# Scores of tiles 3 to 5: two heads on two groups of 64 rows, 128 columns a product, instead of 128 rows with zero halves and 256 columns

## The chip, the cores and the metric

The kernel runs on one core of one Trainium2 chip. The metric is the device time of one execution in microseconds (us), the median of three runs.

## What is computed

A chunked linear attention over 4 batches, 8 heads, 768 positions (head size 32, state size 16), then a gated feed-forward layer (256 to 1536 to 256, with an RMS norm ahead) and a second feed-forward layer (256 to 1024 to 256) that mixes each position with the one before it. Cut to what matters here:

```python
CB = np.einsum('bhin,bhjn->bhij', Cc, Bc)      # the scores
L = np.exp(cum[:, :, :, None] - cum[:, :, None, :]) * causal
M = CB * L
y = np.einsum('bhij,bhjd->bhid', M, xc) + np.einsum('bhin,bhnd->bhid', Cc, state) * decay_to_i
...
x = moe(y, w_gate, w_val, w_out, rms_g)        # silu(x w_gate) * (x w_val) w_out
out = moe2(x, mu_k, mu_r, w_k, w_v, w_r)       # sigmoid(xr w_r) * (relu(xk w_k)^2 w_v)
```

A score sums over only 16 states; it has to be as good as float32.

## The kernel before

The 768 positions are cut into six tiles, 0 to 5, of 128 positions by 4 batches (512 columns). Stage t runs the first feed-forward layer of tile t (12 units of gate, value and output products, names g, v and x) and then the second layer of tile t - 1 (names kp, v, rps). The attention of tile t + 1 is worked in between the units of the first layer, through `attend`. A big product is made of three rounded products (L748, L749, L750: high by high, low by high, high by low), each 128 rows by 128 columns of weights against 512 columns in the rounded float32 type (F32R, the trace writes both float32 types as f32 for TensorE).

Scores come from two functions. `scores` (L468; tiles 0 to 2) uses plain float32, on four groups of 32 rows; a plain float32 product stands in the trace as two records. `scores_r` (tiles 3 to 5) uses F32R, one record a product. For it `terms` splits B and C into a rounded part and a rest, so that a score is the sum of four terms over 16 states, 64 rows for one head. Tile `Br` holds, for a pair of heads, 4 terms x 2 heads x 16 states on 128 rows; ScalarE (L425) and VectorE (L428) turn it into `Bs`. `Cr` becomes `Cs`, which has for each pair two blocks of 128 columns, one for each head, with zeros on the rows of the other head: two ScalarE instructions (L427) and two VectorE ones (L430) with column masks from `shape_constants`. One product of `scores_r` (L442) then takes the 128 rows of a pair and gives 256 columns, the scores of both heads. Four products make one batch, a set; there are 3 tiles x 4 batches = 12 sets. A set fills two PSUM banks of the pool `patt`, heads 0 to 3 in the first and 4 to 7 in the second. `mask` (L514) multiplies each bank with the decays E.

`load_terms` (L418) fetches Br and Cr ahead, one DMA of 128 rows each, on SP's queue; both have two buffers, and `Bs` and `Cs` one. `Cs` takes its place from the tag "Cs", which `mix` (p1, L823) uses too. The tag "rs", of half its size, holds the spread norm of a tile (`rms_mm` to `xn_f`, L730).

Other products on groups of rows or columns: `y_two` (L569) and `y_four` (L594), plain float32 on two groups of 64 rows, 128 columns each; `y_x` (L527) and `y_st` (L533), on groups of 32 output rows; `spread_e` (L393), F32R on groups of 32 rows with 512 columns. `rms_mm` (L685) makes plain float32 products of 128 rows with one column.

The order on each engine is not written by hand: `arrange` at the end plays the program through with a table of prices (`price`) and fixes the order that comes out. An instruction starts there when its inputs, its place and its engine are free, the earliest in the program first.

Of the kernel before, what the change touches and what calls it, by code (L numbers as in the profile page):

```python
# [9 lines left out]
F32 = mybir.dt.float32  # L10
F32R = mybir.dt.float32r
BF16 = mybir.dt.bfloat16
I32, U32 = mybir.dt.int32, mybir.dt.uint32
AF = mybir.ActivationFunctionType
ALU = mybir.AluOpType

P = 128
NB, NH, S, D, N = 4, 8, 768, 32, 16
# [3 lines left out]
T = NB * P  # L22

SB, SC0, SC1, MC0, MC1, EPS = range(6)
# [30 lines left out]
def shape_constants():  # L55
    p = np.arange(P)
    k = np.zeros((P, KW), np.float32)
    k[:, EPS] = 1e-6
    term, h2 = p // 32, (p // 16) % 2
    k[:, SB] = np.where(term >= 2, -1.0, 0.0)  # L60
    for j in range(2):
        k[:, MC0 + j] = h2 == j
        k[:, SC0 + j] = np.where((term % 2 == 1) & (h2 == j), -1.0, 0.0)
    for h in range(NH):
        k[:, M8 + h] = (p // N) % 4 == h
    rest, last, head = p % 4 % 2, p % 4 // 2, p // 4 % NH
    k[:, GL] = np.where(rest == 1, -1.0, 0.0)
    k[:, SL], k[:, CL] = np.where(last == 1, -1.0, 0.0), last == 0
    k[:, SR], k[:, CR] = last == 0, last == 1
    for j in range(2):  # L70
        k[:, ML + j] = head // 4 == j
    for h in range(4):
        k[:, MR + h] = head % 4 == h
    return k
# [3 lines left out]
def tile_kernel(ctx: ExitStack, tc, a_c, x_t, B_t, B_s, C_s, B_p, C_p, C_h, kc,  # L78
                w_gate, w_val, w_out, w_k, w_v, w_r, out):
    nc = tc.nc  # L80
    slots, chains, groups, gates, urgent, ranks, costs = {}, [], [], [], [], {}, {}
# [13 lines left out]
    rp = Pool("rp", 1)  # L95
# [3 lines left out]
    patt = Pool("patt", 2, bass.MemoryType.PSUM)  # L99
# [16 lines left out]
    def f32(ap):  # L116
        return ap.bitcast(F32)
# [39 lines left out]
    def kcol(j):  # L157
        return k_sb[:, j:j + 1]
# [63 lines left out]
    for q in range(NU // 2):  # L222
        s = slice(2 * P * q, 2 * P * (q + 1))
# [81 lines left out]
    A = {c: {} for c in range(NC + 2)}  # L305
# [70 lines left out]
    def spread_eye(c, b):  # L376
        for half in range(2):
            pool, tag = (pacc, "acc") if c and b in LATE_E else (pmm, "mm")
            ps = A[c]["Eb", b, half] = pool.tile([P, T], F32, tag=tag, name="Eb")
            mm = nc.tensor.matmul(ps, eye, before.unsqueeze(1).broadcast_to([P, 4, P]), start=True, stop=False)  # L380
            if len(costs) < COLD:
                costs[mm.ins.name] = 427.0
            A[c]["eye", b, half] = mm.ins.name
# [24 lines left out]
    def parity(c):  # L408
        return c == 2

    def load_terms(c, b):
        if b >= NB:
            c, b = c + 1, b - NB
        if c >= NC:
            return
        for nm, src in (("Br", B_s), ("Cr", C_s)):
            r = A[c][nm, b] = rp.tile([P, T], F32, tag=nm, bufs=2, name=nm)
            nc.sync.dma_start(out=r, in_=src[c, b].unsqueeze(0).broadcast_to([4, 32, T]))  # L418

    def terms(c, b):  # L420
        d = A[c]
        bs = d["Bs", b] = rp.tile([P, 4, P], F32R, tag="Bs", bufs=1, name="Bs")
        cs = d["Cs", b] = rp.tile([P, 4, 2, P], F32R, tag="Cs", bufs=1, name="Cs")
        br, cr = (d.pop((nm, b)).rearrange("p (k i) -> p k i", k=4) for nm in ("Br", "Cr"))
        nc.scalar.activation(out=bs, in_=br, func=AF.Copy, scale=kcol(SB))  # L425
        for j in range(2):
            nc.scalar.activation(out=cs[:, :, j, :], in_=cr, func=AF.Copy, scale=kcol(SC0 + j))  # L427
        nc.vector.tensor_add(bs, br, f32(bs))  # L428
        for j in range(2):
            nc.vector.scalar_tensor_tensor(  # L430
                out=cs[:, :, j, :], in0=cr, scalar=kcol(MC0 + j), in1=f32(cs[:, :, j, :]),
                op0=ALU.mult, op1=ALU.add)
        load_terms(c, b + 2)

    def scores_r(c, b):
        d = A[c]
        bs, cs = d.pop(("Bs", b)), d.pop(("Cs", b))
        for half in range(2):
            bank = d["sc", b, half] = patt.tile([P, T], F32, tag="at", name="sc")
            for q in range(2):  # L440
                p = 2 * half + q
                nc.tensor.matmul(bank[:, q * 256:(q + 1) * 256], bs[:, p, :],  # L442
                                 cs[:, p, :, :].rearrange("p a i -> p (a i)"), start=True, stop=True)

    def load16(r, src):
        for g in range(4):
# [21 lines left out]
    def scores(c, two):  # L468
        br, cr = A[c].pop(("B16", two)) if parity(c) else A[c]["B4"][:, two], A[c].pop(("C4", two))
        pools = ((patt, "at"), (pacc, "acc") if (c, two) in SPARE else (pmm, "mm"))  # L470
        banks = [[pool.tile([P, T], F32, tag=tag, name="sc") for _ in range(2)] for pool, tag in pools]
        rows, w, n = (N, P, 4) if parity(c) else (2 * N, 2 * P, 2)
        for k in range(n):
            for j in range(4):
                g = slice(32 * j, 32 * j + rows)
                mm = nc.tensor.matmul(banks[j // 2][j % 2][:, k * w:(k + 1) * w], br[g, k * P:(k + 1) * P], cr[g, k * w:(k + 1) * w],
                                      start=True, stop=True)
                costs[mm.ins.name] = w / 2.0
                if j + k == 0:
                    groups.append((mm.ins.name, [t.name for bank in banks for t in bank]))  # L480
                A[c]["sc", 2 * two + j // 2, j % 2] = banks[j // 2][j % 2]
        if c and two:
            for two in range(2):
                if c == 1:
                    load_bs(c + 1, two)
                    load_c(c + 1, two, nc.sync)
                else:
                    load_terms(c + 1, two)
# [20 lines left out]
    def mask(c, b, half):  # L509
        d = A[c]  # L510
        if c == 0 and ("M", b) not in d:
            d["M", b] = rp.tile([P, NH, P], F32, tag="hl", bufs=pair_bufs["hl"], name="M")
        s = slice(half, NH, 2) if parity(c) else slice(4 * half, 4 * half + 4)
        nc.vector.tensor_mul(d["E" if c else "M", b][:, s, :], d.pop(("sc", b, half)).rearrange("p (h i) -> p h i", h=4), d["E", b][:, s, :])  # L514

    def masked(c, b):
        decayed_b(c, b)
        for half in range(2):
            mask(c, b, half)
# [373 lines left out]
    def warm_up(n, pool, tag):  # L893
        w = pool.tile([P, T], F32, tag=tag, name="warm")
        for k in range(n):
            mm = nc.tensor.matmul(w, ones, ones.unsqueeze(1).broadcast_to([P, 4, P]), start=True, stop=True)
            if len(costs) < COLD:
                costs[mm.ins.name] = 427.0 if costs else 900.0
# [32 lines left out]
    def masks(b):  # L931
        for half in range(2):
            mask(0, b, half)
# [25 lines left out]
    def late_decayed(_):  # L959
        for b in range(NB):  # L960
# [4 lines left out]
                 k=lambda n: (norm_eye, scan_masks)[n](), w=lambda n: warm_up(n, patt, "at"), q=lambda b: spread_eye(0, b))  # L965
    for step in START.split():
        at = len(list(nc.cur_bb.bb.instructions))
# [27 lines left out]
    for t in range(NC):  # L995
        c, e = t + 1, t + 2
# [25 lines left out]
        def attend(u):  # L1022
# [6 lines left out]
            if c > 2 and u in (1, 3, 6, 8):  # L1029
                terms(c, (u + 1) // 3)  # L1030
            if c > 2 and u in at_sc:
                scores_r(c, at_sc.index(u))
                masked(c, at_sc.index(u))
            elif u in at_sc and (c, at_sc.index(u)) not in SPARE:
                two = at_sc.index(u)
                scores(c, two)
                for b in range(2 * two, 2 * two + 2):
                    masked(c, b)
# [373 lines left out]
```

## Time and profile before

| | us |
|---|---|
| median of 3 runs (lowest, highest) | 508.61 (508.54, 508.73) |
| the profiled execution, its own time | 508.6 |
| its span on the engines | 506.6 |
| TensorE (PE) busy | 500.2 |
| VectorE (DVE) busy | 375.7 |
| ScalarE (ACT) busy | 307.9 |

The 2.0 us between the span and the execution's time lie around the program. Busy time of TensorE counts a product from its start to its modelled end, and products follow each other sooner than that: a product of 512 columns is shown with 389 ns, and the next starts 227 ns later. So the cost of a product is read from the distance of starts or from the chain of waits, not from its own length. The granted clock of TensorE was full (1.00 in every stretch).

### The profile page before, as it was taken

The page shows a single profiled execution, that of the slowest core. Times are in us where ns is not written, and L with a number is a line of the kernel's source. Part 1 is how long each engine was busy: PE and PEld are TensorE (multiplying, and loading weights), DVE is VectorE, ACT ScalarE, POOL GpSimd, SP SyncE. Part 2 cuts the span into 40 slices and gives each one's busy share as a digit, 9 for nine tenths or more (in the row PEclk, how much of TensorE's full clock was granted, in tenths as well). Part 3 has the DMA queues.
Part 4 walks back from the last instruction along what each step waited for, and adds up shares of the span by engine and source line. Part 5 has one row for each costly group of instructions (what it writes and reads, how often), then busy time and mean ns, then how long its engine had stood idle before and what let it go on. Part 6 is the DMA issues. An engine that isn't in the chain of part 4 may idle for free.

```text
span 506.6 us, 7497 instructions
## 1 busy us (share of the span) xinstructions
PE 500.2 (99%) x2869; PEld 406.8 (80%) x2869; DVE 375.7 (74%) x610; ACT 307.9 (61%) x509; POOL 10.4 (2%) x26
## 2 busy tenths in 40 slices
PE   8999999999999999999999999999999999999997
PEld 4687887788888888888888888888888888888885
DVE  6899998988698965479995659996628763335672
ACT  5999798566589744457763456764358643345552
POOL 1100000000010000010000010000000000000000
PEclk9999999999999999999999999999999999999999
DMA  8868755342321220152111141110000000000101
GB/s 257 230 204 276 261 175 193 105 137 93 123 85 43 78 82 13 57 174 77 42 58 68 46 162 44 65 48 36 0 1 1 18 25 1 1 1 0 42 0 42
DMA packets 23283, 42.60 MB, mean 84 GB/s; under 512 B 3136, under 2 KB 6720, under 8 KB 23248
## 3 DMA queue, kind: packets, MB, share of 16 engines
q1 hardware_dynamic: 20496, 33.41, 20.0%
q10 hardware_dynamic: 2752, 8.72, 5.1%
q8 instruction: 22, 0.36, 0.3%
q14 instruction: 13, 0.11, 0.1%
HBM read 38.52 MB, written 3.34 MB: 83 GB/s over the span
## 4 chain that ended last, share of the span: by engine, by line
PE 91%; DVE 5%; ACT 2%; issue 1%; DMA 1%; DVEq 0%; ACTq 0%
PE v L748 10%; PE v L750 10%; PE v L749 10%; PE g L748 6%; PE x L748 6%; PE x L749 6%; PE x L750 6%; PE g L749 6%; PE g L750 6%; PE kp L748 4%; PE kp L750 4%; PE kp L749 4%; PE y L527 2%; PE sc L442 1%; PE rps L750 1%; PE rps L749 1%
## 5 line engine op out<-in xcount | busy, mean ns | idle before, releaser
L792 DVE TENSOR_TENSOR hf<-sl,v 128x512 f32<-128x512 f32 x72 | 49.0, 683 | 50.0 <-PE v L750 49.5
L140 ACT CAST h<-hf 128x512 fp32r<-128x512 f32 x72 | 44.4, 617 | 60.8 <-DVE hf L792 60.7
L133 ACT ACTIVATE sl<-g 128x512 f32<-128x512 f32 x72 | 42.8, 595 | 44.9 <-PE g L750 44.6
L143 DVE TENSOR_TENSOR h<-hf,h 128x512 fp32r<-128x512 f32 x72 | 50.5, 701 | 24.1 <-ACT h L140 24.1
L748 PE MATMUL g<-xn,wgh 128*128 128x512 f32 (+1 forms) x148 | 58.0, 392 | 0.4 <-DVE E L514 0.4
L749 PE MATMUL g<-xn,wgl 128*128 128x512 f32 (+1 forms) x148 | 57.0, 385 | 0.4 <-DVE wgl L289 0.4
L748 PE MATMUL v<-xn,wvh 128*128 128x512 f32 (+1 forms) x148 | 57.0, 385 | 0.0
L750 PE MATMUL g<-xn,wgh 128*128 128x512 f32 (+1 forms) x148 | 56.8, 384 | 0.0
L749 PE MATMUL v<-xn,wvl 128*128 128x512 f32 (+1 forms) x148 | 56.8, 384 | 0.0
L750 PE MATMUL v<-xn,wvh 128*128 128x512 f32 (+1 forms) x148 | 56.8, 383 | 0.0
L749 PE MATMUL x<-h,wol 128*128 128x512 f32 x144 | 56.3, 391 | 0.0
L748 PE MATMUL x<-h,woh 128*128 128x512 f32 x144 | 55.8, 391 | 0.1
L750 PE MATMUL x<-h,woh 128*128 128x512 f32 x144 | 55.2, 389 | 0.0
L867 DVE TENSOR_TENSOR k<-rl 128x512 f32<-128x512 f32 x40 | 30.0, 749 | 15.0 <-ACT rl L863 15.0
L143 DVE TENSOR_TENSOR h<-k,h 128x512 fp32r<-128x512 f32 x48 | 32.8, 686 | 10.3 <-ACT h L140 9.9
L140 ACT CAST h<-k 128x512 fp32r<-128x512 f32 x48 | 29.7, 619 | 16.5 <-DVE k L867 16.3
L748 PE MATMUL kp<-xm,wkh 128*128 128x512 f32 x96 | 37.7, 393 | 0.0
L750 PE MATMUL kp<-xm,wkh 128*128 128x512 f32 x96 | 37.4, 390 | 0.0
L749 PE MATMUL kp<-xm,wkl 128*128 128x512 f32 x96 | 37.4, 389 | 0.0
L748 PE MATMUL v<-h,wvvh 128*128 128x512 f32 x96 | 37.3, 389 | 0.0
L749 PE MATMUL v<-h,wvvl 128*128 128x512 f32 x96 | 37.3, 389 | 0.0
L863 ACT ACTIVATE rl<-kp 128x512 f32<-128x512 f32 x48 | 28.5, 594 | 14.1 <-PE kp L750 13.4
(157 smaller groups left out, 983.0 us busy)
## 6 DMA issues: line engine op xcount, KB each, us to landing
E<-la_r ACTq DMA_DIRECT2D x16, 512.0 KB
x<-in_x_t SPq DMA_DIRECT2D x6, 512.0 KB
wst<-in_w_gate SPq DMA_DIRECT2D x6, 512.0 KB
wst<-in_w_val SPq DMA_DIRECT2D x6, 512.0 KB
wst<-in_w_out SPq DMA_DIRECT2D x6, 512.0 KB
Br<-in_B_s SPq DMA_DIRECT2D x12, 256.0 KB
Cr<-in_C_s SPq DMA_DIRECT2D x12, 256.0 KB
out<-r SPq DMA_DIRECT2D x11, 256.0 KB
```

The lines of the kernel that those rows point to most:

```text
L133: one = nc.scalar.activation(out=out, in_=in_, func=func, **kw).ins.name
L140: last[1] = nc.scalar.copy(x[:, 0, :], src).ins
L143: last[0] = le.tensor_tensor(out=x[:, 1, :], in0=src, in1=f32(x[:, 0, :]), op=ALU.subtract).ins
L442: nc.tensor.matmul(bank[:, q * 256:(q + 1) * 256], bs[:, p, :], cs[:, p, :, :].rearrange("p a i -> p (a i)"), start=True, stop=True)
L527: nc.tensor.matmul(y[half][32 * j:32 * j + 32, at[half]:at[half] + P], x[:, b, h * D:(h + 1) * D], m[:, h, :], start=start and at[half] == ...
L748: nc.tensor.matmul(ps[:, s], w[0][:, k, ws], x[:, 0, s], start=first, stop=False, skip_group_check=s.stop - s.start < T)
L749: nc.tensor.matmul(ps[:, s], w[1][:, k, ws], x[:, 0, s], start=False, stop=False, skip_group_check=s.stop - s.start < T)
L750: nc.tensor.matmul(ps[:, s], w[0][:, k, ws], x[:, 1, s], start=False, stop=last, skip_group_check=s.stop - s.start < T)
L792: nc.vector.tensor_mul(hf, sl, v)
L863: marks.append(nc.scalar.activation(out=rl, in_=kp, func=AF.Relu).ins.name)
L867: nc.vector.tensor_mul(k2, rl, rl)
```

## The change

A head gets its own 64 rows. `load_terms` places 4 terms x 16 states of the pair's first head on rows 0 to 63 and those of the second head on rows 64 to 127, with two DMAs of 64 rows for each of Br and Cr. `terms` treats C as it treats B: one ScalarE and one VectorE instruction each; `Cs` has no zero halves, 512 columns instead of 1024, and lies in the place of tag "rs". `scores_r` makes eight products a set (now L434 of the changed file, where lines are shifted by up to 8): for each pair one on rows 0 to 63 and one on rows 64 to 127, each with 128 columns, into two banks, which are now taken together: the first has the even heads, the second the odd ones. `mask` reads the decays with that step for tiles 3 to 5 as it did for tile 2.

```diff
--- before.py
+++ after.py
@@ -56,11 +56,8 @@
     p = np.arange(P)
     k = np.zeros((P, KW), np.float32)
     k[:, EPS] = 1e-6
-    term, h2 = p // 32, (p // 16) % 2
-    k[:, SB] = np.where(term >= 2, -1.0, 0.0)
-    for j in range(2):
-        k[:, MC0 + j] = h2 == j
-        k[:, SC0 + j] = np.where((term % 2 == 1) & (h2 == j), -1.0, 0.0)
+    term = p // N % 4
+    k[:, SB], k[:, SC0] = np.where(term >= 2, -1.0, 0.0), np.where(term % 2 == 1, -1.0, 0.0)
     for h in range(NH):
         k[:, M8 + h] = (p // N) % 4 == h
     rest, last, head = p % 4 % 2, p % 4 // 2, p // 4 % NH
@@ -415,32 +412,29 @@
             return
         for nm, src in (("Br", B_s), ("Cr", C_s)):
             r = A[c][nm, b] = rp.tile([P, T], F32, tag=nm, bufs=2, name=nm)
-            nc.sync.dma_start(out=r, in_=src[c, b].unsqueeze(0).broadcast_to([4, 32, T]))
+            for h in range(2):
+                nc.sync.dma_start(out=r[64 * h:64 * h + 64], in_=src[c, b, N * h:N * h + N].unsqueeze(0).broadcast_to([4, N, T]))
 
     def terms(c, b):
-        d = A[c]
-        bs = d["Bs", b] = rp.tile([P, 4, P], F32R, tag="Bs", bufs=1, name="Bs")
-        cs = d["Cs", b] = rp.tile([P, 4, 2, P], F32R, tag="Cs", bufs=1, name="Cs")
-        br, cr = (d.pop((nm, b)).rearrange("p (k i) -> p k i", k=4) for nm in ("Br", "Cr"))
-        nc.scalar.activation(out=bs, in_=br, func=AF.Copy, scale=kcol(SB))
-        for j in range(2):
-            nc.scalar.activation(out=cs[:, :, j, :], in_=cr, func=AF.Copy, scale=kcol(SC0 + j))
-        nc.vector.tensor_add(bs, br, f32(bs))
-        for j in range(2):
-            nc.vector.scalar_tensor_tensor(
-                out=cs[:, :, j, :], in0=cr, scalar=kcol(MC0 + j), in1=f32(cs[:, :, j, :]),
-                op0=ALU.mult, op1=ALU.add)
+        for nm, tag, k in (("B", "Bs", SB), ("C", "rs", SC0)):
+            r = A[c].pop((nm + "r", b))
+            s = A[c][nm + "s", b] = rp.tile([P, T], F32R, tag=tag, bufs=1, name=nm + "s")
+            nc.scalar.activation(out=s, in_=r, func=AF.Copy, scale=kcol(k))
+            nc.vector.tensor_add(s, r, f32(s))
         load_terms(c, b + 2)
 
     def scores_r(c, b):
         d = A[c]
         bs, cs = d.pop(("Bs", b)), d.pop(("Cs", b))
-        for half in range(2):
-            bank = d["sc", b, half] = patt.tile([P, T], F32, tag="at", name="sc")
-            for q in range(2):
-                p = 2 * half + q
-                nc.tensor.matmul(bank[:, q * 256:(q + 1) * 256], bs[:, p, :],
-                                 cs[:, p, :, :].rearrange("p a i -> p (a i)"), start=True, stop=True)
+        banks = [patt.tile([P, T], F32, tag="at", name="sc") for _ in range(2)]
+        for p in range(4):
+            i = slice(p * P, p * P + P)
+            for j in range(2):
+                g = slice(64 * j, 64 * j + 64)
+                mm = nc.tensor.matmul(banks[j][:, i], bs[g, i], cs[g, i], start=True, stop=True)
+                if j + p == 0:
+                    groups.append((mm.ins.name, [t.name for t in banks]))
+                d["sc", b, j] = banks[j]
 
     def load16(r, src):
         for g in range(4):
@@ -510,7 +504,7 @@
         d = A[c]
         if c == 0 and ("M", b) not in d:
             d["M", b] = rp.tile([P, NH, P], F32, tag="hl", bufs=pair_bufs["hl"], name="M")
-        s = slice(half, NH, 2) if parity(c) else slice(4 * half, 4 * half + 4)
+        s = slice(half, NH, 2) if c > 1 else slice(4 * half, 4 * half + 4)
         nc.vector.tensor_mul(d["E" if c else "M", b][:, s, :], d.pop(("sc", b, half)).rearrange("p (h i) -> p h i", h=4), d["E", b][:, s, :])
 
     def masked(c, b):
```

On TensorE, at the first set (tile 3, batch 0; sc are scores, g and v the first layer's products of stage 2). Before:

```order
L750 MATMUL v<-xn,wvh 128x512
L748 MATMUL g<-xn,wgh 128x512
L749 MATMUL g<-xn,wgl 128x512
L750 MATMUL g<-xn,wgh 128x512
L748 MATMUL g<-xn,wgh 128x512
L749 MATMUL g<-xn,wgl 128x512
L750 MATMUL g<-xn,wgh 128x512
L442 MATMUL sc<-Cs,Bs 128x256 x4
L748 MATMUL v<-xn,wvh 128x512
```

The same place after:

```order
L744 MATMUL v<-xn,wvh 128x512
L434 MATMUL sc<-Cs,Bs 128x128 x8
L742 MATMUL g<-xn,wgh 128x512
L743 MATMUL g<-xn,wgl 128x512
L744 MATMUL g<-xn,wgh 128x512
L742 MATMUL g<-xn,wgh 128x512
L743 MATMUL g<-xn,wgl 128x512
L744 MATMUL g<-xn,wgh 128x512
L742 MATMUL v<-xn,wvh 128x512
```

The set stands six products of 512 columns earlier, and has eight products for four; on both sides of it stand products of 128 rows, as before. The other eleven sets also stand alone between such products.

On VectorE, the same stretch and the next set (hf, h and xm belong to the feed-forward layers, E<-sc is `mask`, Bs and Cs are `terms`). Before:

```order
L143 TENSOR_TENSOR h<-hf,h 128x512
L430 SCALAR_TENSOR_TENSOR Cs<-Cr,k_sb,Cs 128x4x128 x2
L792 TENSOR_TENSOR hf<-sl,v 128x512
L514 TENSOR_TENSOR E<-sc,E 128x512 x2
L143 TENSOR_TENSOR h<-hf,h 128x512
L792 TENSOR_TENSOR hf<-sl,v 128x512
L428 TENSOR_TENSOR Bs<-Br,Bs 128x512
L430 SCALAR_TENSOR_TENSOR Cs<-Cr,k_sb,Cs 128x4x128
```

The same place after:

```order
L140 TENSOR_TENSOR h<-hf,h 128x512
L786 TENSOR_TENSOR hf<-sl,v 128x512
L508 TENSOR_TENSOR E<-sc,E 128x4x128 x2
L140 TENSOR_TENSOR h<-hf,h 128x512
L423 TENSOR_TENSOR Bs<-Br,Bs 128x512
L423 TENSOR_TENSOR Cs<-Cr,Cs 128x512
```

The first set's Cs is no longer here: it stands in the stage before, ahead of `mix`, since its place is no longer that of p1. From the second set on, one Cs instruction follows Bs instead of two.

## Rows read from the trace of the kernel before

**Rows 1.** The page's first part: busy us, share of the span, instructions.

```profile
PE 500.2 (99%) x2869; PEld 406.8 (80%) x2869; DVE 375.7 (74%) x610; ACT 307.9 (61%) x509; POOL 10.4 (2%) x26
```

**Rows 2.** Who waited for whom from 125 us on: total us, times, longest.

```profile
PEld y L594 <- issue: 1.4, 4, 0.4
PEld sc L442 <- issue: 0.4, 2, 0.2
PEld sc L442 <- DVE Cs L430: 0.3, 1, 0.3
```

**Rows 3.** The chain that ended last, 125 to 506 us: start, us, what.

```profile
131.16 1.09 PE y L594 x16
...
173.37 0.63 PE sc L442 x4
...
256.51 0.47 PE sc L442 x4
...
261.54 0.50 PE sc L442 x4
...
341.12 0.51 PE sc L442 x4
```

**Rows 4.** The same chain around the second set, and at the last.

```profile
180.61 0.23 PE x L750
180.84 0.47 PE sc L442 x4
181.31 0.23 PE g L748
...
365.50 0.47 PE sc L442 x4
```

**Rows 5.** The chain around two products on two groups of 64 rows.

```profile
38.11 0.42 PE y L569 x4
38.53 0.43 PE x L749
```

**Rows 6.** The chain around sixteen products on four groups of rows.

```profile
117.59 1.10 PE sc L476 x32
118.70 0.43 PE g L748
```

**Rows 7.** The chain over eight records of one column with 128 rows.

```profile
75.17 0.45 PE x L748 x2
75.62 0.80 PE ss L685 x8
```

**Rows 8.** TensorE's groups by shape: weights, moving data, count, busy us, mean ns, idle.

```profile
L442 PE MATMUL sc<-Cs,Bs 128*128 128x256 f32 x48 | 7.8, 285 | 0.0
L476 PE MATMUL sc<-Cr,Br 16*128 16x128 f32 x64 | 2.3, 283 | 0.0
L569 PE MATMUL y<-Ch,Sf 64*128 64x128 f32 x16 | 1.7, 310 | 0.0
```

**Rows 9.** Timeline of TensorE's weight loads and products: start, us, shape, [idle before].

```profile
38.04 0.30 PEld L569 LDWEIGHTS y<-Ch,Sf 64*128 64x128 f32 x4 [0.36 <-issue]
...
7.70 0.30 PEld L393 LDWEIGHTS Eb<-wvvh,wkh 32*128 32x128 f32 x4 [0.42 <-issue]
...
7.71 0.73 PE L393 MATMUL Eb<-wvvh,wkh 32*128 32x512 f32 x4
```

**Rows 10.** Instructions of `terms`, `mask` and `load_terms`: ns min/median/max, first and last start.

```profile
L427 ACT ACTIVATE Cs<-Cr,k_sb x24: 707/712/722, 169.8 to 358.6; 128x512 fp32r<-128x512 f32 x24
L430 DVE SCALAR_TENSOR_TENSOR Cs<-Cr,k_sb,Cs x24: 742/745/749, 171.8 to 359.4; 128x512 fp32r<-128x512 f32 x24
L428 DVE TENSOR_TENSOR Bs<-Br,Bs x12: 681/683/686, 109.9 to 358.2; 128x512 fp32r<-128x512 f32 x12
L514 DVE TENSOR_TENSOR E<-sc,E x40: 679/683/692, 25.5 to 366.8; 128x512 f32<-128x512 f32 x40
L418 SPq DMA_DIRECT2D Br<-in_B_s x12: 536/545/580, 96.4 to 338.9; - x12
```

## The prediction

> **What bounds the kernel now.** I read the page's busy times first: TensorE is busy for 500.2 of 506.6 us, VectorE for 375.7, ScalarE for 307.9 [rows 1]. So the question is what TensorE has to do, and whether it ever waits. The first instruction that stands elsewhere on TensorE is the first set of scores of tile 3, at 173 us; of the waits from 125 us on, the products have none, and the weight loads wait for another engine once, 0.3 us: the first set, for VectorE's Cs. The rest is "issue", time in which nothing is waited for, mostly ahead of L594 [rows 2]. So in the stretch that the change touches, the kernel is as long as its queue of products, and a microsecond more or less on TensorE is a microsecond of the result. Work that VectorE, ScalarE or a DMA saves there has nothing to give.
>
> Next I read the chain of waits, which says what each set costs on that path. A usual set of four products of 256 columns takes 0.47 us [rows 4], 0.118 us a product. Three sets took longer, 0.63, 0.50 and 0.51 us [rows 3]; the other nine are at 0.47, from 180.84 to 365.50 us [rows 4]. Twelve sets: 1.64 + 9 x 0.47 = 5.87 us. That is all there is to win on the path.
>
> **The change part by part.**
>
> *The products.* A set becomes four steps of two products, one on each group of 64 rows. Two questions decide: what a step costs, and what going to groups of rows and back costs. Both are in the trace for other products.
>
> L569 is two products on two groups of 64 rows with 128 columns [rows 8], the new shape but in plain float32, two records each: two steps of two. It is alone between products of 128 rows, as the new sets are. The chain gives it 0.42 us, and the product behind it 0.43 instead of 0.23 us [rows 5, 4]: 0.62 us in all. L476 for tile 2 is sixteen products of 128 columns on four groups, 32 records, eight steps of four: 1.10 us, and again 0.43 for the product behind, so 1.30 us [rows 6]. Between them lie six steps: (1.30 - 0.62) / 6 = 0.113 us a step, whether two or four products stand side by side. What is left with no step at all is 0.62 - 2 x 0.113 = 0.39 us: the two changes of the array between 128 rows and groups of rows. The 0.20 us behind are half of it. The other half is ahead: the weight loads of L569 begin 0.36 us after the last load ended, put down to "issue" [rows 9], where they otherwise run during the product before. L594, eight steps of two groups of 64 rows, takes 1.09 us on the chain [rows 3], as L476 does, so the number of groups does not matter.
>
> A new set is then 0.39 + 4 x 0.113 = 0.84, with rounding 0.85 us, against 0.47. Twelve: 10.2 us.
>
> Why does a step not get shorter with fewer columns? L685 has records of 128 rows with one column only, and eight of them take 0.80 us on the chain [rows 7], 0.10 a step. So the step is that of the weight load, and 256 columns at 0.118 us were already near it. A set has eight loads instead of four, two of them at a time. From these rows a step is between 0.10 and 0.113 us; I take 0.113, since it comes from steps with groups and 128 columns. The lower end would take 12 x 4 x 0.013 = 0.6 us off.
>
> The Trainium skill states a lower price: TensorE: Matmul & The Clock Gate, section Back-to-back issue gap, has about 81 ns for a product of 128 columns in a stream of loads and products. By that the twelve sets would be 12 x (0.39 + 4 x 0.081) = 8.6 us and the time 511.3. No row here shows 81 ns with a new float32 weight tile each time; the rows' 0.10 to 0.113 us decide.
>
> One thing no row shows: rounded float32 products with fewer than 256 columns. At 256 they cost 0.118 us. From below, the step cannot be under the 0.10 of the load. From above, such a product could run as plain float32 does, in two passes: a set would then be eight steps, which is exactly L476's 1.30 us. I take the lower value, as the rounded products with 512 and 256 columns both run in one record, and keep the upper one as a rival.
>
> *The first set's wait.* It cost 0.63 - 0.47 = 0.16 us for Cs. The order now has this Cs in the stage before, and the set six products earlier with Bs made long before; the wait goes. It is in the 5.87 already. The extra 0.03 and 0.04 us of two other sets I don't expect back.
>
> *ScalarE and VectorE.* ScalarE loses one instruction of 712 ns a set, 8.5 us in twelve. VectorE has 683 ns instead of 2 x 745, 9.7 us less [rows 10]. TensorE waits for neither after 173 us, so this is worth nothing. What hides it is the queue of products itself. `mask` keeps its length: the 40 instructions of L514, eight of them with the step of two heads already, lie between 679 and 692 ns [rows 10].
>
> *The two banks together.* A set now needs both banks of `patt` free at its first product. The first two sets of tile 3 stand 7.5 us apart and those of tile 4, the closest of all, 5.0 us [rows 3, 4]; the two masks between them take 1.4 us [rows 10]. Nothing.
>
> *The loads.* 48 issues for 24. If one of half the size takes SP's queue as long, some 0.55 us [rows 10], that is 13 us more of it, spread over the 240 us from 96 to 339 us, with the same bytes. Queued behind them are x, Ch, the decays and the output tiles. The transfers are asked for a set or more ahead, and all but the last outputs have a stage's time; the last ones come after the last of these loads. Nothing, and if a load came late, ScalarE's Bs would be late first, as it was once before.
>
> *The tag "rs".* Cs of the first set must wait until the norm of the tile before has been read; that is at the end of the second layer's units, ahead of Cs in the new order too. Nothing.
>
> Sum: 10.2 - 5.87 = +4.3 us, all on TensorE. The profiled execution took 508.6 us, span 506.6 and 2.0 around it, and the median is 508.61, so one sum serves both: **512.9 us**.
>
> **The rivals.**
>
> *Half rate at 128 columns (or one group after the other).* If rounded products under 256 columns run as plain float32, or if the two groups do not run side by side, a set has eight steps: 12 x 1.30 - 5.87 = +9.7, **518.3 us**. For the first speaks only that the kernel before put zeros in to reach 256 columns, which is no measurement. Against the second, L393: four rounded products on groups of 32 rows lie within 0.73 us, though each has 512 columns, 0.23 us on the chain when alone [rows 9, 4]: four in a row would need 0.9 us.
>
> *No price for changing groups, in this type.* The 0.39 us comes from plain float32 sets between rounded products. If it belonged to the change of type and not of rows, a new set would be 4 x 0.113 = 0.45 us: 12 x 0.45 - 5.87 = -0.5, **508.1 us**, not slower. This is the case on the other side. It decides once the two changes together cost under 0.04 us (5.87 / 12 = 0.49, less 0.45) instead of 0.39. Against it: L685 is plain float32 too, with 128 rows, and it follows two products at 0.45 us with 0.80 us for its eight loads and no more; and L393, rounded and on groups, follows a product of 128 rows in another type with a gap of 0.42 us [rows 7, 9]. The Trainium skill, TensorEngine Tiling (Array Packing), section Key Properties, ties the drain to the change of tiling mode; no row here shows it between two rounded products.
>
> *Half the time.* If a step cost what its columns do, half of 0.118, with no price for the change, a set would be 0.24 us: 12 x 0.24 - 5.87 = -3.0, **505.6 us**. The Trainium skill, TensorEngine Tiling (Array Packing), section Theoretical Speedup, gives up to 2x for a contraction of 64 or fewer. Against it stands the 0.10 us of a step with a single column [rows 7].
>
> *It doesn't relieve anyone.* A gain through the freed VectorE and ScalarE is excluded by the waits [rows 2]; a new wait by the moved order is possible, at the turn of the stages, where VectorE is fullest, and would add some tenths each.
>
> **How the numbers follow.** Forecast 0.62; eight steps a set 0.24 (0.18 the type, 0.06 the groups); no price for the change 0.07; half the time 0.04; something slower that I don't see 0.03. The likeliest gives 512.9. Its own range is 512.2 (a step of 0.10) to 513.6 (0.06 us more a set, from the rounding of the chain and a tenth here and there). That alone holds six in ten, so the range goes on to the eight steps, 518.3, with the same tenths on top: 512.2 to 518.8. About 0.2%, 1.0 us, is what a measurement of this kernel can tell from no change: faster 0.04, the same 0.07, slower 0.89.
>
> **What would show it.** Right: 96 records of 64 rows by 128 columns at the scores; on the chain 0.65 us for eight of them (0.19 + 4 x 0.113) and 0.43 for the product behind; twelve new "issue" waits of some 0.36 us on the weight loads, as L594 has four now; ScalarE and VectorE 8 to 10 us less busy, with the waits of TensorE as before. Eight steps: 1.1 us on the chain, or 192 records. No price: 0.45 us and no "issue" row. Wrong altogether: a wait of TensorE for VectorE, ScalarE or a DMA from 165 us on, or a granted clock below full around the sets.

## The result and the profile after

The changed kernel took 513.31 us (median; 512.42 to 516.01), the kernel before, beside it on the same chip, 508.67 us (508.54 to 508.74). The kernel after takes 1.009 times the kernel before by these medians (513.31 / 508.67), and 1.01 times by the means of four executions each; the 95% interval of the latter is 1.0061 to 1.014. The forecast was 512.9, in a range from 512.2 to 518.8, with 0.89 on slower. So it was right on which way and in its range, and the distance to the median is 0.4 us. Part of that nearness is luck: the set of products came out cheaper than forecast, and a low clock in two of the four executions made up for it, as the next rows show.

The page of after: the span, then busy time, share and instructions of each engine ([rows 1] before), and of the 40 slices the granted clock of TensorE, 9 for 90% or more.

```profile
span 513.9 us, 7603 instructions
...
PE 507.0 (99%) x2917; PEld 407.9 (79%) x2917; DVE 367.9 (72%) x598; ACT 301.7 (59%) x497; POOL 10.4 (2%) x26
...
PEclk9799999999999999999999999999999999999999
```

TensorE has 6.8 us more, VectorE 7.8 and ScalarE 6.2 less. Not all of the 6.8 is the change: the second slice has a clock of 0.7, and `by_group` below, with the same products at full clock, has TensorE busy for 503.8 us, 3.6 more than before. The windows of after say where (busy time of each engine with its instructions, granted clock, DMA share, GB/s):

```profile
12.00:16.00 4.00, 4.00 (x51) 2.69 (x52) 0.78 (x3) 2.99 (x7) 1.52 (x4) 0.62 1.10 360
16.00:20.00 4.00, 3.89 (x58) 1.98 (x54) 3.66 (x9) 3.48 (x11) 0.00 (x0) 0.81 0.76 175
20.00:24.00 4.00, 3.81 (x46) 2.87 (x47) 2.59 (x9) 2.35 (x9) 0.00 (x0) 0.76 0.74 221
...
125.00:513.00 388.00, 385.36 (x2106) 315.93 (x2104) 258.37 (x408) 208.36 (x339) 6.64 (x6) 1.00 0.14 48
```

In before all of these are at 1.00. From 12 to 24 us parts of after run at the lower of the clock's two levels (1.2 instead of 2.4 GHz), some 150 us ahead of the first instruction that the change moves on TensorE; from 125 us on the clock is full. The four executions of after had mean clocks of 0.993 (516.01 us, the profiled one), 0.996 (513.87), 0.999 (512.42) and 1.000 (512.75). Some executions of either kernel have such a mean clock below full and take 0.5 to 8 us more, and the ratios given here leave out those that lie more than 1.5% above the fastest of their kernel. What the change itself costs is read from 125 us on, and from executions at full clock.

The waits of TensorE's weight loads in after from 125 us on (engine, line, waited for: us in total, times, longest), which answer to [rows 2]:

```profile
PEld sc L434 <- issue: 4.2, 12, 0.4
PEld y L588 <- issue: 1.4, 4, 0.4
PEld kp L742 <- issue: 0.2, 1, 0.2
```

The products have no row at all. There are twelve waits of 0.35 us for nothing that the profile shows, one a set (before had two of 0.2), and the wait for VectorE's Cs is gone. The scores themselves, by their line (duration min/median/max in ns, first and last start in us, forms):

```profile
L434 PE MATMUL sc<-Cs,Bs x96: 272/273/323, 175.5 to 372.9; 64*128 64x128 f32 x96
```

96 records of 64 rows by 128 columns: one record each, so no second pass. And the chain of after around the second set and at the last (start, us, what), which answers to [rows 4]:

```profile
184.38 0.23 PE x L744
184.60 0.59 PE sc L434 x8
185.19 0.42 PE g L742
185.62 0.23 PE g L743
...
372.56 0.59 PE sc L434 x8
373.15 0.42 PE g L742
```

All twelve sets read alike: 0.59 us for eight products, and the product behind at 0.42 instead of 0.23. A set costs 0.59 + 0.19 = 0.78 us where the forecast had 0.85. Twelve are 9.4 us, and 9.4 - 5.87 = **+3.5 us** on the path, not +4.3. Executions at full clock agree within some tenths: after 511.99 to 512.88, before, beside them, 508.3 to 508.9, some +3.8. (The chain rounds to two digits. From the starts of the records, third product ahead of each set to ninth behind it, the twelve differ by +3.7.)

### The profile page after: what moved, and what is told of

It is laid out like the page before. It is cut to its first block, busy times and chain, and to the rows that moved or that the text cites. A ratio compares the mean times of both kernels' runs of the same rounds, so it can differ in the third digit from the quotient of the medians.

```text
span 513.9 us, 7603 instructions
## 1 busy us (share of the span) xinstructions
PE 507.0 (99%) x2917; PEld 407.9 (79%) x2917; DVE 367.9 (72%) x598; ACT 301.7 (59%) x497; POOL 10.4 (2%) x26
## 4 chain that ended last, share of the span: by engine, by line
PE 90%; DVE 5%; ACT 2%; issue 1%; DMA 1%; ACTq 0%; DVEq 0%
PE v L742 10%; PE v L744 10%; PE v L743 10%; PE g L742 6%; PE x L742 6%; PE x L743 6%; PE x L744 6%; PE g L743 6%; PE g L744 6%; PE kp L742 4%; PE kp L744 4%; PE kp L743 4%; PE y L521 2%; PE sc L434 1%; PE rps L743 1%; PE rps L744 1%
## 5 line engine op out<-in xcount | busy, mean ns | idle before, releaser
L742 PE MATMUL g<-xn,wgh 128*128 128x512 f32 (+1 forms) x148 | 59.2, 400 | 0.4 <-DVE E L508 0.4
L744 PE MATMUL g<-xn,wgh 128*128 128x512 f32 (+1 forms) x148 | 56.9, 385 | 0.0
## 6 DMA issues: line engine op xcount, KB each, us to landing
E<-la_r ACTq DMA_DIRECT2D x16, 512.0 KB
x<-in_x_t SPq DMA_DIRECT2D x6, 512.0 KB
wst<-in_w_gate SPq DMA_DIRECT2D x6, 512.0 KB
wst<-in_w_val SPq DMA_DIRECT2D x6, 512.0 KB
wst<-in_w_out SPq DMA_DIRECT2D x6, 512.0 KB
```

Of the source, the lines that this page charges most:

```text
L742: nc.tensor.matmul(ps[:, s], w[0][:, k, ws], x[:, 0, s], start=first, stop=False, skip_group_check=s.stop - s.start < T)
L744: nc.tensor.matmul(ps[:, s], w[0][:, k, ws], x[:, 1, s], start=False, stop=last, skip_group_check=s.stop - s.start < T)
```

## The experiments

The theory, called A in the expectations, is the prediction's: TensorE's queue of products is the time; a step costs its weight load, about 0.112 us, whatever its columns; two products on two groups share a step; a visit of the array to groups of rows costs about 0.35 us on top. The letters of rivals are spelled out where they come.

**The same kernel again, and the kernel before against itself.** `after_again` and `before_copy` carry no edit.

> The changed kernel once more, beside the kernel before on the same chip. Theory A (each set costs 0.79 us on TensorE's path instead of 0.48, by the trace of after, and nothing else changes): 508.6 + 12 x 0.31 = 512.3 us in runs with a granted clock of 1.000, and the kernel before at 508.6. Rival B (the drop of the granted clock in the first 25 us, seen in the profile of after, belongs to the change): most runs of the changed kernel lie above 513 with a mean clock under 0.998, and none of before does. Rival C (that drop is chance): it is seen in a run or two of either kernel.

Nine executions: median 512.88 (511.99 to 520.26), before 508.63 in 22; ratio 1.0086 (1.0054 to 1.0117). The five at a clock of 1.000 lie between 511.99 and 512.88, the four others (0.980 to 0.993) between 515.23 and 520.26. Of the 22 of before beside them two had a clock below 0.998 (510.05 and 513.6 us). So neither B's "most runs, and none of before" nor C's "a run or two of either" is what came.

> The kernel before, unchanged, in the place of a changed one. Theory C (the drop of the granted clock in the first 25 us comes by chance, in any kernel): some executions with a mean clock below 0.998 and 1 to 8 us more here too, the others at 508.3 to 508.9. Rival B (it belongs to the changed kernels): none.

508.68 (508.32 to 510.13) against 508.62; ratio 1.0006 (0.9996 to 1.0017). Five of its twelve executions had a clock of 0.996 to 0.998 (509.12 to 510.13 us), and four of the 17 of before beside it, one of them 0.980 with 516.49. So the low clock comes without any edit, as theory C has it, and needs no part of the change. Whether the changed kernel falls into it more often (four of nine against two of 22 on one chip) is not settled by so few.

**The loads and rows alone.** The kernel before with the new placing of rows and the split DMAs, but its old products:

```diff
-    term, h2 = p // 32, (p // 16) % 2
+    term, h2 = p // 16 % 4, p // 64
...
-            nc.sync.dma_start(out=r, in_=src[c, b].unsqueeze(0).broadcast_to([4, 32, T]))
+            for h in range(2):
+                nc.sync.dma_start(out=r[64 * h:64 * h + 64],
+                                  in_=src[c, b, N * h:N * h + N].unsqueeze(0).broadcast_to([4, N, T]))
```

> The kernel before with only the new rows and loads: a head's 4 terms x 16 states on its own 64 rows, two DMAs of 64 rows for each of Br and Cr; zero halves, four products of 128 rows by 256 columns a set and the old banks stay. Theory A: 508.6 us, within 0.3. If the split loads or SP's 24 more issues cost something, it lies above 509.5. Rival B, with the loads as its cause: granted clock under 0.998 in most runs.

508.8 us; ratio 1.0003 (0.9981 to 1.0025). Twice as many loads on SP's queue cost nothing that can be measured here. Four of the twelve executions had a clock under 0.998 (0.979 to 0.997), not most, so rival B is not borne out for the loads. What the changed kernel takes longer does not come from the loads or the rows.

**Each pair of products twice.** Four more steps a set, no further visit:

```diff
-            for j in range(2):
+            for n in range(4):
+                j = n % 2
```

> The changed kernel with each pair of products made twice in a row (eight steps a set instead of four; the second overwrites the first with the same values). Theory A (a step costs its weight loads, 0.112 us): 12 x 4 x 0.112 = 5.4 us above the changed kernel, 517.7 against 512.3. Rival D (a step costs its 128 columns, half of 0.118 us, and the rest of the set's 0.79 us is the change between row groups): 12 x 4 x 0.059 = 2.8 us above, 515.1.

517.78 us (517.51 to 519.27); ratio 1.0175 (1.0131 to 1.022). The chain, twelve times alike:

```profile
172.18 1.04 PE sc L435 x16
173.22 0.42 PE g L743
```

(1.04 - 0.59) / 4 = 0.112 us a step, and the product behind stays at 0.42: the visit is paid once, a step each time. 48 steps more are 5.4 us, as the times say.

**Twice the columns.** Six of the eight products write 256 columns, all but those of the last step; the columns that they write too many are written again by the next step:

```diff
-                mm = nc.tensor.matmul(banks[j][:, i], bs[g, i], cs[g, i], start=True, stop=True)
+                w = slice(p * P, min(p * P + 2 * P, T))
+                mm = nc.tensor.matmul(banks[j][:, w], bs[g, i], cs[g, w], start=True, stop=True)
```

> The changed kernel with 256 columns in six of a set's eight products (each takes its pair's columns and the next pair's, whose places the next product overwrites), still on two groups of 64 rows. Theory A (the weight load sets the step): within 0.4 us of the changed kernel, 512.3 to 512.7, since 256 columns take no longer than the load. Rival D (the columns set it): three steps a set by 0.059 us more, 12 x 3 x 0.059 = 2.1 us above, 514.4.

513.03 us (512.53 to 513.32; at full clock 512.53 to 512.81); ratio 1.0076 (1.0049 to 1.0103). The chain:

```profile
172.92 0.61 PE sc L435 x8
173.53 0.43 PE g L743
```

0.61 and 0.43 for 0.59 and 0.42: in six products 128 columns more each cost 0.03 us together, little more than the rounding of the chain, where rival D wanted 0.18. So between 128 and 256 columns the step hardly depends on the columns; that it is the weight load's is what fits, with the 0.10 us of a single column [rows 7]. Every product here has its own load, so no run tells the load's price from that of the product's own start.

**One load more a product, no groups.** The kernel before with each of its four products of 256 columns cut into two of 128, on 128 rows with the zero halves:

```diff
-                nc.tensor.matmul(bank[:, q * 256:(q + 1) * 256], bs[:, p, :],
-                                 cs[:, p, :, :].rearrange("p a i -> p (a i)"), start=True, stop=True)
+                for j in range(2):
+                    nc.tensor.matmul(bank[:, q * 256 + j * P:q * 256 + (j + 1) * P], bs[:, p, :],
+                                     cs[:, p, j, :], start=True, stop=True)
```

> The kernel before with each product of 128 rows by 256 columns cut into two of 128 columns on all 128 rows (the same weights loaded twice): eight products a set, no row groups. Theory A (a step costs its weight load, 0.112 us, whatever the columns): 12 x (8 x 0.112 - 0.48) = 5.0 us above the kernel before, 513.6. Rival D (columns set the step): the same columns as before, 508.6.

514.11 us (514.01 to 515.05); ratio 1.0106 (1.009 to 1.0122), +5.5; twelve sets at 0.90 would be +4.9, but in this order five of them stand in two pieces. The chain around one in one piece:

```profile
181.20 0.23 PE x L751
181.43 0.84 PE sc L443 x8
182.27 0.29 PE g L749
182.56 0.23 PE g L750
```

0.84 + 0.06 = 0.90 us for eight steps, 0.11 each, and next to nothing behind: here the array keeps its 128 rows. Half the columns made no product shorter. With this the change can be taken apart: four more loads, 0.90 - 0.47 = +0.43 us a set; two loads at a time, 4 x 0.112 = -0.45; the visit, 0.78 - 0.45 = +0.33. The sum is +0.31: what the groups save, the additional loads had cost, and the visit is left over.

**Two visits a set.** Two steps where the set stands, the other two three products later, chained behind the gate's last product:

```diff
-        for p in range(4):
+        for p in (2 * part, 2 * part + 1):
...
+        def between(u):
+            if c > 2 and c < NC and u in at_sc:
+                scores_r(c, at_sc.index(u), 1)
+                masked(c, at_sc.index(u))
```

> The changed kernel with each set cut in two: pairs 0 and 1 before a unit's gate and value products, pairs 2 and 3 behind its last gate product or later. The same 96 products, but 24 visits to the row groups instead of 12. Theory A (a visit costs its two changes, 0.79 - 4 x 0.112 = 0.35 us, and 0.112 a step): 12 x 0.35 = 4.2 us above the changed kernel, 516.5 against 512.3. Rival E (no price for changing groups; the set's longer time comes from the products themselves): 512.3, unchanged.

516.86 us (the executions at full clock 516.64 to 516.86); ratio 1.0158 (1.014 to 1.0176), +4.4 over after at full clock. The chain of one half, and the wait from 125 us on:

```profile
179.96 0.37 PE sc L437 x4
180.33 0.43 PE g L749
```

```profile
PEld sc L437 <- issue: 8.5, 24, 0.4
```

(The profiled execution had the low clock, from 11 to 32 us; these rows lie behind that, at 1.00.) A half costs 0.37 + 0.20 = 0.57 us, two of them 1.14 against 0.78: a visit more is 0.36 us, with the same 96 products, and shows one more wait for "issue" of 0.35. So it is going to groups of rows and back that costs, between rounded products too. The Trainium skill (TensorEngine Tiling (Array Packing), Key Properties) ties the drain to the change of tiling mode without a price; the trace agrees as far as it goes: the weight loads stand idle for 0.35 us at each visit, and a visit costs 0.33 to 0.36 us.

**The four products of one group first.** The loops are exchanged, so that the queue holds four products on rows 0 to 63 and then four on 64 to 127:

```diff
-        for p in range(4):
-            i = slice(p * P, p * P + P)
-            for j in range(2):
-                g = slice(64 * j, 64 * j + 64)
+        for j in range(2):
+            g = slice(64 * j, 64 * j + 64)
+            for p in range(4):
+                i = slice(p * P, p * P + P)
```

> The changed kernel with the products of a set in another order: the four on rows 0 to 63 first, then the four on rows 64 to 127. Theory A (two products share a step only when neighbours in the queue are on different groups): about eight steps a set, 12 x 4 x 0.112 = 5.4 us above the changed kernel at most, 517 to 517.7. Rival F (the groups run on their own whatever the order): 512.3, unchanged.

512.49 us (512.33 to 512.68); ratio 1.007 (1.0056 to 1.0085). Here A's expectation, some 517 us, was wrong, and the rival F, that each group goes on by itself whatever the order, was right. The chain:

```profile
180.93 0.60 PE sc L434 x8
181.53 0.43 PE g L742
...
368.88 0.60 PE sc L434 x8
```

0.60 us, not the 1.04 of eight steps one after another. In the trace the starts of the eight products are 180.855, 180.868, 181.018, 181.031, 181.132, 181.143, 181.243 and 181.257 us: still four pairs, 11 to 14 ns apart instead of 3. That the queue really held four and four shows in the semaphore that the products raise. In after the two products of a set's last pair raise it by several and by one; here both raise it by several, so each closes a row of its own. Products on different rows ran side by side although the queue did not alternate.

This profile also settles what the profiled execution of after lost at its start. Its sets stand in the same places, the second at 180.93 and the last at 368.88 us, against 184.60 and 372.56 in after: 3.67 and 3.68 later. So from the second set to the last the two took the same time, and the 3.7 us by which after's span is longer (513.9 against 510.2) lie ahead of the sets, where after's clock was low.

**The last step with 256 columns.** The columns of a last step have no later load to hide them. Were they what made the forecast's set too long?

```diff
-                mm = nc.tensor.matmul(banks[j][:, i], bs[g, i], cs[g, i], start=True, stop=True)
+                w = slice(2 * P, T) if p == 3 else i
+                mm = nc.tensor.matmul(banks[j][:, w], bs[g, i], cs[g, w], start=True, stop=True)
```

> The changed kernel with 256 columns instead of 128 in the last pair's two products of each set alone; they also write over the place of the pair before, whose scores (heads 4 and 5 of tiles 3 to 5) are then not the reference's. Theory A' (a set is its three steps of 0.112, the changes of the array, and the columns of the last step, which no load hides: 0.053 us for 128 and 0.107 for 256): a set of 0.65 us on the chain instead of 0.59, 12 x 0.054 = 0.6 us above the changed kernel, 512.9 against 512.3. Theory A as predicted (every step costs its load, the last one too): unchanged, 0.59 us on the chain.

513.61 us (513.37 to 514.4), and 513.37 and 513.38 at full clock, +4.8 on before at full clock (508.4 to 508.7 beside it); ratio 1.0087 (1.006 to 1.0113). The chain:

```profile
181.28 0.23 PE x L745
181.50 0.65 PE sc L435 x8
182.15 0.43 PE g L743
```

0.65 + 0.20 = 0.85 us, as much as the set that was forecast. So 128 columns more in the last step cost 0.06 us, in the six other products together 0.03 (`cols256`). The twelve sets of this chain come to +4.3 us; 0.5 us of the measured +4.8 is in no row.

**Rounded sets for tile 2 too.** If a set of tile 2 in plain float32 costs 1.30 us [rows 6] and a rounded one of before 0.47, could tile 2 change over as well? In the kernel before, with the order numbers that tile 3 has:

```diff
-SCORES = ((4, 7), (3, 8), (2, 4, 8, 10))
-VALUES = ((5, 6, 8, 10), (4, 6, 9, 11), (9, 10, 11, 12))
+SCORES = ((4, 7), (2, 4, 8, 10), (2, 4, 8, 10))
+VALUES = ((5, 6, 8, 10), (9, 10, 11, 12), (9, 10, 11, 12))
...
-        return c == 2
+        return False
...
-            if c > 2 and u in (1, 3, 6, 8):
+            if c > 1 and u in (1, 3, 6, 8):
```

> The kernel before with tile 2's scores made as those of tiles 3 to 5 (F32R, four sets of four products of 128 rows by 256 columns) instead of two plain float32 sets of eight steps on four groups of rows. Theory A (TensorE's queue is the time, a change of groups included): 2 x 1.31 - 4 x 0.48 = 0.7 us less, 507.9. Rival G (in stage 1 VectorE is busy for 9 of 10 us with the weights, and four sets of terms bring 8.7 us more to it and as much to ScalarE, so TensorE comes to wait): 509.5 or more.

520.04 us (518.15 to 524.14); ratio 1.0215 (1.0181 to 1.0248): the time and the waits came as rival G has them. The waits of the products from 70 to 185 us, and the window from 125 to 185 of this kernel and, below it, of before:

```profile
PE g L744 <- ACT sl L133: 3.9, 1, 3.9
PE ss L681 <- ACT sq L658: 1.8, 1, 1.8
```

```profile
125.00:185.00 60.00, 56.09 (x335) 45.61 (x334) 48.47 (x77) 44.14 (x74) 1.53 (x2) 0.94 0.26 87
125.00:185.00 60.00, 60.00 (x365) 49.69 (x364) 51.84 (x81) 43.90 (x74) 2.40 (x2) 1.00 0.24 82
```

In before the products wait for ScalarE nowhere in that stretch. Here they wait 5.7 us for it, and the clock falls behind each wait: from 80 to 90 us it is 0.77, after ten us with products for 8.21, and from 140 to 150 us 0.70, after ten with 7.12. G's reason, more work on VectorE and ScalarE, is not shown: in the window VectorE is busy for less and ScalarE for 0.24 us more than in before. The run also moves when the values of tile 2 are made, and which of the two makes ScalarE late it does not tell. This order only was tried; a better one for tile 2 stays open. No version ran faster than the kernel before.

## Why the prediction came out as it did

*What bounds the kernel:* right. TensorE's products wait for no one from 125 us on, before and after, and the runs that changed only the products of tiles 3 to 5 followed the chain within 0.6 us.

*The step of 0.113 us:* right, 0.112 by `double`, with 0.11 on 128 rows by `full128` and next to no difference between 128 and 256 columns by `cols256`. The Trainium skill's 81 ns (TensorE: Matmul & The Clock Gate, Back-to-back issue gap) does not agree with the trace. An estimate of a set with it and the measured visit of 0.33 us is 0.65; the chain has 0.78.

*The price of changing groups:* the mechanism right, the term mis-sized. The prediction took 0.62 - 2 x 0.113 = 0.39 us from L569, plain float32, and added it unchanged to a rounded set. Measured are 0.78 - 4 x 0.112 = 0.33, and 12 x 0.07 = 0.8 us of the forecast's +4.3 did not come. What was overlooked is that such a remainder also holds the columns of the last step, which no later load covers, and that plain float32 takes longer over them. The trace shows where: from the last weight load of a visit to the next load behind it are 0.307 us at L569 (0.309 at L594), but 0.262 at a set of after, all with 128 columns. With twice the columns in the last step, in `last256`, it is 0.318, and the set takes the 0.85 us of the forecast. So 0.045 of the 0.06 us lie there, as if a record of plain float32 passed its columns at about half the pace. That is an inference from these three distances; no run made the same set in both types.

*Why the median still lies 0.4 us above the forecast:* the profiled execution had the low clock at its start, and one more of the four a mean clock of 0.996 (where in it is not known). At full clock the time is 512.0 to 512.9, and the sum that the chain of after supports gives 508.6 + 3.5 = 512.1. The forecast lay 0.8 us above that; the low clock in two of four executions took the median past it. The 0.4 us is thus two errors that nearly cancel.

*A single record at 128 columns:* right; the range's upper end, 518.3, was bought for it and was not needed. The rival of half rate, at 0.24, was the wrong place for so much chance. L393, which spoke against serial groups, spoke rightly.

*ScalarE, VectorE, the loads, both banks, the tags at nothing:* right in that nobody was relieved. The instructions of `terms` became shorter by 8.6 and 9.7 us, as forecast; the busy time of ScalarE fell by only 6.2 and that of VectorE by 7.8 us, and where the rest went was not followed up; `old_products` shows the loads at nothing.

*The first set's wait for Cs:* gone, as the waits show, and it gained the 0.16 us that the 5.87 held. The extra 0.03 and 0.04 did not come back either.

*The rival on the other side* (no price in this type): excluded by the twelve "issue" waits, by 0.42 us behind each set, and by `split`.

What stays open: why the clock falls early in some executions, and whether the change makes it likelier. In after's profile a weight load waits 0.9 us for the transfer of a Br of the first tiles, against 0.2 in before. That wait ends at 6.5 us, ahead of the fall, so it is no consequence of it; and the fall does not need it, since in `split`, whose clock was at 0.50 from 12 to 28 us, the same load waited 0.2 us as in before, and in `after_again` it has no row. Open too are the tenths by which times at full clock lie above the sums of the chain.

## What to carry to other kernels

With products as short as these, count weight loads, not columns: where every product brought new float32 weights, a step took 0.11 to 0.12 us on 64 or on 128 rows and with 128 or 256 columns. So half the columns saved nothing and twice the loads was the bill, unless groups of rows took them two at a time. A visit of rounded products to groups of rows cost 0.33 to 0.36 us among products of 128 rows, three steps' worth: collect as much work on groups as a visit can hold, or stay at 128 rows and pay with zeros. When a price is taken from a neighbour of another type, ask which of its columns nothing covers, and take those out first.

## What the hardware showed unasked

Products on different groups of rows need not alternate in the queue to run side by side: four on one group ahead of four on the other took 0.60 us, in turn 0.59. Columns cost next to nothing where another load follows, and cost where none does: 128 more in the last step took 0.06 us, in the six products ahead of it 0.03 together. And some executions have a lower clock than others of the same program, of the unchanged kernel too: mean clocks of 0.980 to 0.998 with times 0.5 to 8 us longer. Of the unchanged kernel none of these was profiled; in `after`, `after_again`, `cols256` and `split` the clock fell between 10 and 17 us and was full again by 32 us.
